# Splitting one batch's result rows 32 to 96 instead of 22 to 106 in an FFT filter and cos-gated MLP kernel

## The chip, the cores and the metric

The kernel runs on one core of a Trainium2 chip. A core has a matrix engine (TensorE, PE in the profile), a vector engine (VectorE, DVE), a scalar engine (ScalarE, ACT), a general one (GpSimd, POOL) and a sync engine (SyncE, SP) that here only issues transfers. Each engine works through its own list of instructions in the order in which the list was built and waits at an instruction until what it needs is there; nothing behind it can pass. Transfers (DMAs) are issued by SP and ACT, in this kernel, and carried out by 16 DMA engines that the two queues share. On-chip memory (SBUF) has 128 partitions. The metric is the device time of one execution in microseconds; less is better.

## The reference, cut to what matters

The input x has 8 batches of 3008 rows by 256 channels. First each batch is filtered along its rows in the frequency domain, then every row goes through a two-layer network with a cosine gate:

```python
X = np.fft.rfft(x, axis=1)                      # 8 x 1505 x 256
Y = X * (filt_r + 1j * filt_i)[None]
y = np.fft.irfft(Y, n=3008, axis=1)             # 8 x 3008 x 256
x = y.reshape(24064, 256)
h = x @ w_in                                    # 256 -> 2048
g = h * np.cos(h)
out = g @ w_out                                 # 2048 -> 256
```

All inputs and the output are float32.

## The kernel before, in words

The transform of length 3008 = 47 x 64 is done by matrix products in four stages. Stage 1 transforms along 47, stages 2 and 3 along 64 (with the filter between them), stage 4 along 47 back. Between the stages the data goes through device memory, because the axis that lies on the partitions changes. `z2` is the array between stages 3 and 4: 8 x 32 blocks (index j) of 96 rows by 256 channels. A unit of stage 4 is up to five half blocks (48 rows each). The list of units begins 5, 5, 1, 5, 5, ..., so the first three units are 11 half blocks and give the 512 rows of the network's first chunk; `n_first` is 3, and `units[n_first][0]` is 11, the half block at which unit 3 begins.

The network works on 47 chunks of 512 rows. For each chunk there are eight steps over the hidden width: `hidden` (L466) multiplies by two 128-wide slices of w_in into the PSUM tile `hp`, of which there are two; `gate` (L476 to L483) forms h cos(h) on VectorE and ScalarE and splits it into a high and a low part, `gh` and `gl`, so that fast fp32r products keep the precision; `project` (L495) multiplies by w_out into the accumulators `acc`. The step after next can write into `hp` only once the gate of the step has read it for the last time, in L479.

The weights come from memory as float32 and are split into such pairs on the chip by `prep_w`: SP loads the tile `raw` (L222; 512 KB, three buffers), ScalarE makes `o` and `r` from it (L231, L233), VectorE `t` (L234), GpSimd joins them (L235), ScalarE casts the high part (L238), GpSimd subtracts for the low part (L239). There are 16 such loads, w_in and w_out by turns for steps 0 to 7. Seven are issued during the first batch's transform, two more (w_out for step 3, w_in for step 4) right after the first chunk's stage 4 loads, and the other seven, beginning with w_out for step 4, while the first chunk is computed.

The first batch is special: nothing else can run until the first chunk's rows exist, so its transform is done in plain float32 in `first1` and `first23`. In the latter, twelve pieces of columns end as a tile `z2t` of 128 partitions by 512 numbers (2 KB a partition). Partition p holds rows of half block p/2, so that 22 partitions are the 11 half blocks of units 0 to 2. Those partitions are written to `z2` at once, by ScalarE's queue (L409). The rest is written by the generator's last step (L412), by SP's queue. That step is run for all twelve pieces in one go, after the stage 4 loads of units 0 to 2 and the two weight loads, and is tied by `issue_after` to the last of those stage 4 loads.

The order of each engine's list is found when the program is built: a scheduler with a timeline of its own costs places the instructions by priority and expected readiness; only the SP engine's order in the first batch is taken as written. `run_due` spreads the next batches' stages over the slots of the network's steps. A change of one transfer's shape can thus reorder instructions far from it.

Of the kernel before, what the change touches and what calls it, by code (L numbers as in the profile page):

```python
# [138 lines left out]
def _units():  # L139


    sizes = [5, 5, 1] + [5] * 99 + [3, 3]
    assert sum(sizes) == B * NB
    starts = np.concatenate([[0], np.cumsum(sizes)])
    return [(int(a), int(n)) for a, n in zip(starts, sizes)]
# [10 lines left out]
def fft_filter_then_cos_glu(ctx: ExitStack, tc: tile.TileContext, ins, outT):  # L156
# [41 lines left out]
    units = _units()  # L198
# [4 lines left out]
    n_first = len(of_chunk[0])  # L203
# [57 lines left out]
    def psum_f(b):  # L261
        if b == 0 and len(done) < n_first:
            if not spare:
                spare.extend(ps_h.tile([P, 2, 512], F32, name="hp")[:, u] for u in range(2))
                spare.append(ps_f.tile([P, 512], F32, name="ps", tag="ps"))
            return spare.pop(0)
        return ps_f.tile([P, 512], F32, name="ps", tag="ps")
# [115 lines left out]
    def first23(i, fas, fbs):  # L383
        cols = slice(512 * i, 512 * i + 512)
        zf = fft.tile([P, 512], F32, name="zf", tag="ld", bufs=5)
        nc.sync.dma_start(zf, z1s[0].rearrange("j (h c k) d -> (j h c) (k d)", h=2, c=2)[:, cols])
        yield
        ps = psum_f(0)
        nc.tensor.matmul(ps, mats["f2"], zf, start=True, stop=True)
        half = slice(2 * (i % 2), 2 * (i % 2) + 2)  # L390
        ya = fft.tile([P, 512], F32, name="ya", bufs=2)
        yb = fft.tile([P, 512], F32, name="yb", tag="sw", bufs=2)
        for y, f in ((ya, fas), (yb, fbs)):
            nc.vector.tensor_tensor(y, ps, f[i // 2][:, half].rearrange("p k d -> p (k d)"), ALU.mult)
        yield
        ps = psum_f(0)
        if i == 0:
            for m, c in (("30", slice(0, D)), ("3", slice(D, 512))):
                nc.tensor.matmul(ps[:, c], mats["f" + m], ya[:, c], start=True, stop=False)
                nc.tensor.matmul(ps[:, c], mats["f" + m + "i"], yb[:, c], start=False, stop=True)  # L400
        else:
            nc.tensor.matmul(ps, mats["f3"], ya, start=True, stop=False)
            nc.tensor.matmul(ps, mats["f3i"], yb, start=False, stop=True)
        tag, bufs = at2[i]
        z = fft.tile([P, 512], F32, name="z2t", tag=tag, bufs=bufs)
        nc.scalar.copy(z, ps)
        to = z2[:NJ].rearrange("j (h c k) d -> (j h c) (k d)", h=2, c=2)[:, cols]
        n0 = 2 * units[n_first][0]
        nc.scalar.dma_start(to[:n0], z[:n0])  # L409
        yield  # L410
        wrote2.setdefault(0, []).append(i)
        nc.sync.dma_start(to[n0:], z[n0:])  # L412
# [112 lines left out]
    with tc.tile_pool(name="first", bufs=12) as first, tc.manual_schedule(engines={mybir.EngineType.SP}):  # L525
        fas, fbs, load, sign = filters(first)
        ones = [first1(i, first) for i in range(NJ // 4)]
        twos = [first23(i, fas, fbs) for i in range(n23)]
        for g in ones:
            next(g)  # L530
# [159 lines left out]
```

## Time and profile before

| what | value |
| --- | --- |
| time, median of 3 runs | 2562.18 us (2557.64 to 2562.96) |
| time of the profiled execution | 2562.1 us |
| its span, first to last instruction | 2560.3 us |
| TensorE busy | 2455.7 us, 96% |
| VectorE busy | 1885.4 us, 74% |
| GpSimd busy | 1430.5 us, 56% |
| ScalarE busy | 1286.1 us, 50% |
| mean granted TensorE clock | 0.979 |

The page gives each engine's busy time as a share of the whole span. From 420 us on TensorE is busy nearly all the time; the gaps are all in the first 420 us, so the views that matter are those of stretches of that part: how busy each engine is there, which engine waits for which, and what SP's and ScalarE's queues issue when. A line that names `SPq` is the time an issuing instruction took on SP's sequencer, not the time its data took to move. In the lists of transfers the second column is that issue time, and KB is the size of one transfer.

### The profile page before, as it was taken

The numbers are of one execution on the slowest core, as the hardware profiler recorded it, in microseconds if no ns is written. First come the engines' busy times: TensorE is split into PE (matmuls) and PEld (weight loads), VectorE is DVE, ScalarE is ACT, GpSimd is POOL, SyncE is SP. The second block draws the span as 40 slices with busy tenths as digits, with TensorE's granted clock in tenths as the row PEclk, the third lists the DMA queues.
The fourth block names the chain that finished last, engine by engine and source line by source line (L and its number), as shares of the span: only waits on it lengthen the run. The fifth ranks groups of instructions, "written<-read, shape, count | busy, mean of one in ns | idle before, by whom it ended". The sixth has DMA issues, their size and how long they took to land.

```text
span 2560.3 us, 29873 instructions
## 1 busy us (share of the span) xinstructions
PE 2455.7 (96%) x10783; PEld 1967.7 (77%) x10783; DVE 1885.4 (74%) x1911; ACT 1286.1 (50%) x1707; POOL 1430.5 (56%) x826
## 2 busy tenths in 40 slices
PE   7369889999999999999999999999999999999999
PEld 2257767888888888888888888888888888888887
DVE  2177987888678877888668886787768886666665
ACT  1355564555545555555545555455554554444443
POOL 1366664656656565656546665566555554444443
PEclk8679999999999999999999999999999999999999
DMA  9253342322322232222313223222312211000000
GB/s 318 72 166 89 129 144 65 119 82 82 85 83 91 90 91 71 93 90 78 93 47 105 86 85 85 79 94 74 100 43 88 99 54 48 24 21 9 17 9 17
DMA packets 134749, 212.27 MB, mean 83 GB/s; under 512 B 12521, under 2 KB 64281, under 8 KB 134601
## 3 DMA queue, kind: packets, MB, share of 16 engines
q1 hardware_dynamic: 82385, 137.97, 17.7%
q10 hardware_dynamic: 52216, 72.39, 8.8%
q8 instruction: 86, 1.41, 0.2%
q14 instruction: 62, 0.51, 0.1%
HBM read 135.33 MB, written 74.97 MB: 82 GB/s over the span
## 4 chain that ended last, share of the span: by engine, by line
PE 82%; DVE 7%; DMA 3%; issue 3%; SPq 2%; ACT 2%; POOL 1%; POOLq 0%; ACTq 0%; DVEq 0%
PE hp L466 36%; PE acc L495 36%; PE ps L435 3%; PE ps L251 2%; PE ps L252 2%; PE ps L253 2%; SPq L412 2%; DVE g L476 1%; DMA xf<-in_x 1%; DVE sw L325 1%; DVE g L477 1%; DMA raw<-in_w_in 1%; ACT g L478 1%; DVE g L479 1%; DVE xo L280 1%
## 5 line engine op out<-in xcount | busy, mean ns | idle before, releaser
L483 POOL TENSOR_TENSOR gl<-g,gh 128x1024 fp32r<-128x1024 f32 x376 | 910.7, 2422 | 825.6 <-ACT gh L481 510.7
L466 PE MATMUL hp<-y,w_in 128*128 128x512 f32 x4512 | 1132.6, 400 | 65.8 <-DVE g L479 63.8
L466 PEld LDWEIGHTS hp<-y,w_in 128*128 128x128 f32 x4512 | 845.3, 190 | 266.6 <-issue 59.8
L495 PE MATMUL acc<-gh,w_out 128*128 128x512 f32 x3008 | 896.9, 396 | 0.7 <-ACT gh L481 0.7
L479 DVE TENSOR_TENSOR g<-g,hp 128x1024 f32<-128x1024 f32 x376 | 457.9, 1218 | 320.6 <-ACT g L478 320.1
L478 ACT ACTIVATE g<-g,half_pi 128x1024 f32<-128x1024 f32 x376 | 433.4, 1153 | 484.2 <-DVE g L477 436.6
L495 PEld LDWEIGHTS acc<-gh,w_out 128*128 128x128 f32 x3008 | 564.0, 188 | 131.1 <-ACT gh L481 1.1
L481 ACT CAST gh<-g 128x1024 fp32r<-128x1024 f32 x376 | 394.9, 1051 | 430.5 <-DVE g L479 424.1
L476 DVE TENSOR_SCALAR g<-hp 128x1024 f32<-128x1024 f32 x376 | 458.8, 1220 | 137.7 <-PE hp L466 130.3
L495 PE MATMUL acc<-gl,w_out 128*128 128x512 f32 x1504 | 549.9, 400 | 1.3 <-POOL gl L483 1.3
L477 DVE SCALAR_TENSOR_TENSOR g<-g,hp 128x1024 f32<-128x1024 f32 x376 | 458.0, 1218 | 9.9
L495 PEld LDWEIGHTS acc<-gl,w_out 128*128 128x128 f32 x1504 | 283.7, 189 | 66.7 <-POOL gl L483 2.1
L452 POOL TENSOR_TENSOR y<-y,y 128x470 fp32r<-128x470 f32 (+29 forms) x142 | 124.9, 884 | 55.8 <-ACT y L449 55.8
L435 PEld LDWEIGHTS ps<-m,z 120*128 120x128 f32 (+1 forms) x816 | 129.3, 192 | 21.0
L314 POOL TENSOR_TENSOR zl<-zf,zh 128x512 fp32r<-128x512 f32 x84 | 111.7, 1330 | 47.8 <-DVE zh L313 24.5
L331 POOL TENSOR_TENSOR yl<-ya,yh 128x512 fp32r<-128x512 f32 x84 | 113.2, 1348 | 42.1 <-ACT yh L330 42.0
L435 PE MATMUL ps<-m,z 120*128 120x120 f32 (+1 forms) x816 | 129.2, 273 | 0.0
L325 DVE SCALAR_TENSOR_TENSOR sw<-sw,sg,f 128x256 f32<-128x256 f32 x168 | 116.9, 735 | 0.0
L313 DVE CAST zh<-zf 128x512 fp32r<-128x512 f32 x84 | 93.1, 1108 | 23.1 <-DMA zf<-z 13.4
L327 DVE TENSOR_TENSOR ya<-ya,sw 128x512 f32<-128x512 f32 x84 | 98.5, 1173 | 0.0
L330 ACT CAST yh<-ya 128x512 fp32r<-128x512 f32 x84 | 51.8, 618 | 91.0 <-DVE ya L327 90.7
L449 ACT CAST y<-y 128x470 fp32r<-128x470 f32 (+29 forms) x150 | 66.9, 456 | 41.3 <-DVE y L443 38.9
(96 smaller groups left out, 1413.3 us busy)
## 6 DMA issues: line engine op xcount, KB each, us to landing
z<-z SPq DMA_DIRECT2D x101, 240.0 KB
out_t<-o ACTq DMA_DIRECT2D x94, 256.0 KB
f<-in_fb SPq DMA_DIRECT2D x84, 256.0 KB
f<-in_fa SPq DMA_DIRECT2D x84, 256.0 KB
zf<-z SPq DMA_DIRECT2D x84, 256.0 KB
z<-z2t ACTq DMA_DIRECT2D x84, 256.0 KB
xf<-in_x SPq DMA_DIRECT2D x42, 480.0 KB
z<-z1t ACTq DMA_DIRECT2D x84, 240.0 KB
```

Source lines behind the costliest of these rows:

```text
L325: nc.vector.scalar_tensor_tensor(sw[:, ks], sw[:, ks], sg[:, 2 * i + k : 2 * i + k + 1], fbt[:, ks], ALU.mult, ALU.mult)
L331: nc.gpsimd.tensor_tensor(yl, ya, yh.bitcast(F32), ALU.subtract)
L435: nc.tensor.matmul(v[:, t, a * r : (a + 1) * r], zf[:, a, t * P : (t + 1) * P], mats[f"m4{a}"][:r, :r], start=True, stop=True)
L452: (nc.vector if i < 2 * n_first else nc.gpsimd).tensor_tensor(yl, part, yh.bitcast(F32), ALU.subtract)
L466: nc.tensor.matmul(hp[:, u], w_in[s][w][:, t, fs], y[:, t], start=(t == 0 and n == 0), stop=(t == NDT - 1 and n == 2))
L476: nc.vector.tensor_scalar(g, h, 0.25, MAGIC, ALU.add, ALU.add)
L477: nc.vector.scalar_tensor_tensor(g, g, MAGIC, h, ALU.subtract, ALU.subtract)
L478: nc.scalar.activation(g, g, AF.Sin, bias=half_pi, scale=-TWO_PI)
L479: nc.vector.tensor_tensor(g, g, h, ALU.mult)
L481: nc.scalar.copy(gh, g)
L483: nc.gpsimd.tensor_tensor(gl, g, gh.bitcast(F32), ALU.subtract)
L495: nc.tensor.matmul(acc, w_out[s][w][:, u, es], g[:, u], start=(s == 0 and u == 0 and n == 0), stop=(s == NFT // 2 - 1 and u == 1 and n == 2))
```

## The change

One number changes. `n0` is the count of partitions of each `z2t` tile that are written at once:

```diff
         to = z2[:NJ].rearrange("j (h c k) d -> (j h c) (k d)", h=2, c=2)[:, cols]
-        n0 = 2 * units[n_first][0]
+        n0 = 32
         nc.scalar.dma_start(to[:n0], z[:n0])
         yield
         wrote2.setdefault(0, []).append(i)
         nc.sync.dma_start(to[n0:], z[n0:])
```

Before, `n0` is 2 x 11 = 22, and 106 partitions are left for L412. After, 32 are written at once by L409, which are the half blocks of units 0 to 3, and 96 are left for L412. The bytes written in all are the same.

Because the scheduler places instructions by expected readiness, the order of the engines' lists changes too. SP's list, from the last two deferred writes on (z_112 is the array `z2`, `z2t` the tile that is written, z_619 and the following ones are the tiles of stage 4's units 3, 4, ..., f the filter tiles, raw the weights before their split). Before:

```order
L412 DMA z_112<-z2t 106x512 [waits DMAHW0_49]
L412 DMA z_112<-z2t 106x512 [waits DMAHW1_49]
L222 DMA raw<-in_w_out 128x2x512 [waits DMAHW2_49,Activation_49]
L306 DMA f<-in_fb 128x512 [waits DMAHW3_49]
L307 DMA f<-in_fa 128x512 [waits DMAHW4_49]
L306 DMA f<-in_fb 128x512 [waits DMAHW5_49]
L307 DMA f<-in_fa 128x512 [waits DMAHW6_49]
L306 DMA f<-in_fb 128x512 [waits DMAHW7_49]
L222 DMA raw<-in_w_in 128x2x512 [waits DMAHW0_49,Activation_49]
L307 DMA f<-in_fa 128x512 [waits DMAHW1_49]
L222 DMA raw<-in_w_out 128x2x512 [waits DMAHW2_49,Activation_49]
L425 DMA z_619<-z_112 120x2x256 [waits DMAHW3_49,PE_49]
```

With the change:

```order
L412 DMA z_112<-z2t 96x512 [waits DMAHW1_49]
L425 DMA z_619<-z_112 120x2x256 [waits DMAHW2_49,PE_49]
L222 DMA raw<-in_w_out 128x2x512 [waits DMAHW3_49,Activation_49]
L306 DMA f<-in_fb 128x512 [waits DMAHW4_49]
L307 DMA f<-in_fa 128x512 [waits DMAHW5_49]
L306 DMA f<-in_fb 128x512 [waits DMAHW6_49]
L307 DMA f<-in_fa 128x512 [waits DMAHW7_49]
L222 DMA raw<-in_w_in 128x2x512 [waits DMAHW0_49,Activation_49]
L306 DMA f<-in_fb 128x512 [waits DMAHW1_49]
L222 DMA raw<-in_w_out 128x2x512 [waits DMAHW2_49,Activation_49]
L425 DMA z_624<-z_112 120x2x256 [waits DMAHW3_49,PE_49]
```

Unit 3's load (z_619), which came after three weight loads and six filter loads, now stands ahead of the first of them; unit 4's (z_624) stands behind three weight loads, as before. The twelve deferred writes keep their place.

TensorE's list, from the end of the network's step 1 (`hp` with w_in_1) to its step 2 (`hp` with w_in_2). Before:

```order
L466 MATMUL hp<-y_555,w_in_1_82 128x512
L466 MATMUL hp<-y_554,w_in_1_83 128x512
L466 MATMUL hp<-y_554,w_in_2_84 128x512 [waits DVE_49,PE_49]
L466 MATMUL hp<-y_555,w_in_2_84 128x512
L466 MATMUL hp<-y_554,w_in_2_85 128x512 [waits Pool_49]
```

With the change (z_619 and z_624 are stage 4 of units 3 and 4, into a PSUM tile `ps` each):

```order
L466 MATMUL hp<-y_554,w_in_1_83 128x512
L435 MATMUL ps<-m_310,z_619 128x120 [waits DMAHW2_49]
L435 MATMUL ps<-m_312,z_619 128x120
L435 MATMUL ps<-m_310,z_619 128x120
L435 MATMUL ps<-m_312,z_619 128x120
L435 MATMUL ps<-m_310,z_624 128x120 [waits DMAHW3_49]
L435 MATMUL ps<-m_312,z_624 128x120
L435 MATMUL ps<-m_310,z_624 128x120
L466 MATMUL hp<-y_554,w_in_2_84 128x512 [waits DVE_49,PE_49]
```

Stage 4 of unit 3 and most of unit 4's now stand between steps 1 and 2, where before step 2 came first and the two units after it. Further on, the lists of all engines differ in the places of single instructions as well.

## The prediction

> **What bounds the kernel now.** I read the stretches first: the busy time of each engine, with the granted clock, the mean busy share of the 16 DMA engines and GB/s in the last three columns.
>
> ```profile
> core 0: us, PE busy (x) PEld busy (x) DVE busy (x) ACT busy (x) POOL busy (x), PEclk, DMA share, GB/s
> 80.00:100.00 20.00, 13.59 (x48) 11.20 (x48) 4.65 (x13) 7.11 (x16) 9.97 (x8) 0.67 0.26 94
> 100.00:120.00 20.00, 0.00 (x0) 0.00 (x0) 0.00 (x0) 0.00 (x0) 0.00 (x0) 0.50 0.13 51
> 120.00:140.00 20.00, 0.00 (x0) 0.00 (x0) 2.65 (x3) 1.83 (x3) 1.38 (x2) 0.50 0.55 192
> 160.00:200.00 40.00, 34.12 (x133) 25.97 (x132) 38.65 (x36) 22.74 (x37) 34.41 (x20) 0.91 0.39 105
> 200.00:300.00 100.00, 97.64 (x441) 78.57 (x440) 83.87 (x86) 53.21 (x75) 65.78 (x40) 1.00 0.36 110
> 300.00:420.00 120.00, 106.14 (x438) 82.46 (x437) 98.63 (x99) 65.57 (x96) 74.72 (x46) 0.94 0.41 123
> 500.00:2560.00 2060.00, 2053.43 (x9182) 1668.59 (x9180) 1556.03 (x1556) 1057.32 (x1364) 1159.12 (x656) 1.00 0.23 70
> ```
>
> After 500 us TensorE is busy 2053 of 2060 us: there it is the bound, and time won before it shifts all of it. Between 100 and 120 us no engine computes at all, and the DMA engines run at 0.13 of their capacity, which is two of sixteen. What keeps them so is in SP's list (start, time of the issuing instructions, count) and in the transfers of that stretch:
>
> ```profile
> 78.62 0.40 SPq L222 DMA_DIRECT2D raw<-in_w_in  x1
> 79.06 43.36 SPq L412 DMA_DIRECT2D z<-z2t  x12
> 122.52 4.30 SPq L222 DMA_DIRECT2D raw<-in_w_out  x1
> ```
>
> ```profile
> DMA packets 509, 1.02 MB, mean 51 GB/s; under 512 B 10, under 2 KB 10, under 8 KB 509
> z<-z2t SPq DMA_DIRECT2D x5, 212.0 KB
> ```
>
> The deferred writes of 106 partitions hold SP for 43.36 us. All twelve are 12 x 106 x 2 KB = 2.61 MB, which at 51 GB/s takes 51 us; SP is held nearly that long, because a new write cannot be issued before the queue has room. Only then comes the next weight load, w_out for step 4. Who waits for it stands in the waits of 76 to 145 us and in ScalarE's and TensorE's rows (the bracket is the idle time before the row, and what ended it):
>
> ```profile
> PE hp L466 <- DVE g L479: 48.2, 1, 48.2
> DVE t L234 <- ACT o L231: 47.4, 2, 47.0
> ACT o L231 <- DMA raw<-in_w_out: 44.6, 2, 44.1
> ```
>
> ```profile
> 91.79 0.62 ACT L238 CAST w_in<-o 128x512 fp32r<-128x512 f32 x1 [1.26 <-POOL o L235]
> 136.55 0.66 ACT L231 ACTIVATE o<-raw 128x512 f32<-128x512 f32 x1 [44.14 <-DMA raw<-in_w_out]
> ```
>
> ```profile
> 87.29 8.27 PE L466 MATMUL hp<-y,w_in 128*128 128x512 f32 x24 [1.97 <-ACT y L449]
> 143.80 4.58 PE L466 MATMUL hp<-y,w_in 128*128 128x512 f32 x12 [48.24 <-DVE g L479]
> ```
>
> Read backwards: TensorE has done steps 0 and 1 (24 products) and needs an `hp` tile back; that hangs on the gate of step 0; in VectorE's list the gate stands behind the weight split's L234, which waits for ScalarE's L231, which waits for the weights, which stand behind the writes in SP's queue. One transfer at the head of SP's list holds four engines. ScalarE is free at 91.79 + 0.62 = 92.41 us and starts at 136.55; TensorE follows 143.80 - 136.55 = 7.25 us later.
>
> **The change part by part.** What is added: the writes at once grow from 22 to 32 partitions. Their count (twelve), place and issuing instructions are the same; they run while the queues are nearly empty. The stage 4 loads of the first chunk wait for the last of them:
>
> ```profile
> 76.63 1.28 SPq L425 DMA_DIRECT2D z<-z  x3
> ```
>
> ```profile
> GB/s 30 0 0 0 0 0 0 0 0 0 0 0 15 179 134 0 0 0 0 0 0 0 0 0 0 0 0 45 149 134 0 0 0 0 0 0 0 0 0 0
> ```
>
> The second row is 72 to 77.5 us in forty slices: the last two writes are the two bursts, and the last burst ends after 30 slices, at 76.1 us, 0.5 us before the waiting load goes out.
>
> I leave that start where it is: 20 KB more is 0.4 us even at the 51 GB/s of two engines, and on more engines less; I take 0, between -0.4 and 0.4.
>
> What is made smaller: 12 x 96 x 2 KB = 2.36 MB in deferred writes. The trace of before has no deferred write of 96 partitions, so I look for the nearest rows: how many engines does a 96-partition tile get? From 3 to 7 us only the loads of 96x512 tiles run on SP's queue, and from 24 to 28 us mostly ScalarE's writes of 96-partition tiles to memory (queue q10):
>
> ```profile
> q1 hardware_dynamic: 616, 1.08, 94.1%
> xf<-in_x SPq DMA_DIRECT2D x8, 192.0 KB
> ```
>
> ```profile
> DMA packets 1246, 1.51 MB, mean 377 GB/s; under 512 B 62, under 2 KB 1150, under 8 KB 1246
> q10 hardware_dynamic: 1132, 1.11, 78.8%
> ```
>
> Both keep all sixteen engines busy (94.1%; 78.8% for q10 with q1 filling the rest). So I expect the deferred writes on all sixteen engines, at 377 GB/s: 2.36 / 0.377 = 6.3 us in place of 51 us. The lower bound is the two engines of now (51 GB/s, 46 us); in between, the rate when the stage 4 and weight loads run together, 255 GB/s:
>
> ```profile
> 79.00:84.00 5.00, 4.28 (x19) 4.07 (x19) 1.39 (x4) 3.15 (x7) 4.39 (x5) 0.50 0.86 255
> 130.00:135.00 5.00, 0.00 (x0) 0.00 (x0) 0.00 (x0) 0.00 (x0) 0.00 (x0) 0.50 0.95 342
> ```
>
> ```profile
> GB/s 0 0 5 87 128 108 353 364 343 261 210 261 215 174 256 144 148 195 241 389 358 369 379 430 358 420 389 420 369 287 164 62 31 51 51 51 51 51 51 51
> ```
>
> The last row is 77 to 85 us in forty slices of 0.2 us: what is queued before the writes has drained after 31 of them, at 83.2 us. From there:
>
> - writes 6.3 us: 89.5 us
> - unit 3's load, now first: 245 KB at the 342 GB/s of the second row: 0.7 us
> - w_out for step 4: 524 KB at 342 GB/s: 1.5 us, so 91.7 us; with the 0.5 us from data to release seen above: 92.2 us.
>
> ScalarE is busy until 92.41 us anyway. Its wait of 44.14 us is then gone and the order of the chain behind it (L231, L234, the two gates' L476 and L477, L238, L478, L479) is as before: step 2 could begin at 92.4 + 7.25 = 99.7 us.
>
> What is moved: seven products of units 3 and 4 now stand ahead of step 2. Rows of ScalarE and TensorE that bear on it:
>
> ```profile
> 87.82 0.68 ACT L233 ACTIVATE r<-raw 128x512 int32<-128x512 uint32 x1
> 88.97 0.67 ACT L233 ACTIVATE r<-raw 128x512 int32<-128x512 uint32 x1
> ```
>
> ```profile
> 148.22 1.94 PE L435 MATMUL ps<-m,z 120*128 120x120 f32 x16
> ```
>
> Unit 3's data is there by 91 us. Unit 4's load is issued behind four filter loads, w_in 5, one more filter load and w_out 5. Those two weight loads wait for `raw` buffers that ScalarE frees by 88.5 and 89.6 us (the two L233 rows, w_out 3 and w_in 4), so they wait for nothing later. Five filter loads of 262 KB, two weights of 524 KB and unit 4's 245 KB are 2.6 MB, 7.6 us at 342 GB/s: 91.7 + 7.6 + 0.5 = 99.8 us, then three products, 3 x 1.94/16 = 0.4 us, doubled for a slow clock: 0.8 us. Step 2 begins at 100.6 us instead of 143.80: **43.2 us** less. Bounds: if nothing is late, 143.80 - 99.7 = 44.1 us; at 255 GB/s all along, the writes take 9.3, the two loads 3.0 and the next 2.6 MB 10.2 us, unit 4 lands at 83.2 + 22.5 + 0.5 = 106.2 us and step 2 begins at 107.0, a gain of 36.8 us.
>
> Behind that, two small terms. Of the sixteen stage 4 products at 148.22 us seven are done in the idle time: 0.8 us. And w_in 6, for which ScalarE waited, need not be as late:
>
> ```profile
> 152.05 0.68 ACT L231 ACTIVATE o<-raw 128x512 f32<-128x512 f32 x1 [3.90 <-DMA raw<-in_w_in]
> ```
>
> Of these 3.90 us I take 1, between 0 and 3.9, as TensorE was not idle at that place and only what follows on VectorE gains. The clock gives nothing: step 2 was slow (4.58 us for 12 products, where twelve of the 24 of steps 0 and 1 take 4.1, also after an idle stretch) and will still come after an idle stretch of some 4 us, and a gap of 1.99 us at 167.49 us already had the same price:
>
> ```profile
> 167.49 4.59 PE L466 MATMUL hp<-y,w_in 128*128 128x512 f32 x12 [1.99 <-DVE g L479]
> ```
>
> What is reordered: from 160 to 420 us VectorE is nearly full (38.65 of 40 us in the first of these rows) and TensorE idles 5.9 + 2.4 + 13.9 = 22.1 us. The work there is the same and starts earlier; its new order may win or lose some of these 22 us. Between -22 (all gone) and +22 (twice as much) I take 0, with 8 either way as likely.
>
> Sum: 43.2 + 0.8 + 1.0 = 45.0 us from the profiled execution's 2562.1 us (span 2560.3 and 1.8 around it), and that execution stands 0.1 us from the median: 2517 us.
>
> On the count of engines the Trainium skill has two voices, both in DMA: Bandwidth & Descriptors. Its table "Specifications" gives eight partitions per engine as a convention; by that 106 partitions would lie on fourteen engines, the slowness would have another cause, and the change would only save bytes, the time of rival B below. Its section "Why a DMA increments its semaphore by 16 and not by 1" has the largest divisor up to 16 of the outer dimension decide: 106 gives two, 96 sixteen. The trace's 0.13 agrees with the second and contradicts the first.
>
> **The rivals.**
>
> A, the forecast: 2517 us, its own range 2508 to 2527.
>
> B, the change doesn't widen the writes: they are slow because of their target or pattern, and 96 partitions cost 96/106 of 106. Then SP is held 43.36 x 96/106 = 39.3 us, 4 us less, and the time is 2558. For it: no write of just this shape is in the trace. Against it: two engines' share exactly, and 96-partition writes at 377 GB/s.
>
> C, the wait goes over to the next weights: SP comes to them 37 us earlier, but they then stand in one burst with filters and unit loads, and steps 4 to 6 wait for w_out 4 to w_in 6 one after another. If each of the four loads is late by the 3.90 us of the row above, 15.6 us are given back: 2533. Against it: the queue has 2.6 MB then, 7.6 us, while TensorE needs w_in 5 only for the fourth step from there.
>
> D, the crowded stretch of 160 to 420 us loses as much as it idles now: 22 us back, 2539. For it: VectorE at 97% there, and a new order on all engines. Against: the same work in the same stretch, with more transfers done ahead.
>
> E, slower: TensorE's list now has unit 4 ahead of step 2. If its load is caught behind w_in 5 and w_out 5, whose buffers ScalarE must free, and that ScalarE work stood behind the gates, every microsecond is TensorE's. It decides from a landing at 143 us; with 151 us, 8 us worse than now, the time is 2570. Against: ScalarE's rows that free the buffers are over at 89.6 us, before any gate.
>
> **How the numbers follow.** A 0.83, B 0.03, C 0.07, D 0.05, E 0.02. The likeliest gives 2517 us. The range, 2506 to 2530, takes in the 8 us of reordering below and above, and above it the slow rate's 36.8 us in place of 43.2. About 0.2% (5 us) is what a measurement of this kernel can tell from no change. A, C and D are faster, 0.95; B is within, 0.03; E is slower, 0.02.
>
> **What would show it.** Right: the L412 rows together take some 8 us or less on SP; the stretch after 83 us shows the DMA engines near full; ScalarE's wait before w_out 4 is under 3 us; step 2 of TensorE begins near 101 us, after products of units 3 and 4; TensorE is full from about 375 us on. Wrong: L412 still above 30 us (B); TensorE's waits move to L222's weights (C); its idle time between 120 and 380 us well above 22 us (D); a long wait of L435 for z ahead of step 2 (E).

## The result, and the profile after

The changed kernel takes 2517.2 us, median of 4 runs (2516.79 to 2519.81), beside 2561.74 us for the kernel before: a ratio of 0.9831, 95% interval 0.9814 to 0.9848. The profiled execution took 2516.79 us with a span of 2515.0 us; the span is 45.3 us shorter.

SP's list of the changed kernel (start, time of the issuing instructions, count):

```profile
78.69 0.40 SPq L222 DMA_DIRECT2D raw<-in_w_in  x1
79.14 8.40 SPq L412 DMA_DIRECT2D z<-z2t  x12
87.66 1.01 SPq L425 DMA_DIRECT2D z<-z  x1
88.77 0.57 SPq L222 DMA_DIRECT2D raw<-in_w_out  x1
```

The twelve deferred writes hold SP for 8.40 us where they held it 43.36 us, and the next weight load goes out at 88.77 us, 33.75 us earlier than before (122.52). The transfers of the changed kernel from 84 to 89 us (packets, MB, share of sixteen engines in the second row):

```profile
DMA packets 1087, 1.92 MB, mean 384 GB/s; under 512 B 153, under 2 KB 153, under 8 KB 1086
q1 hardware_dynamic: 1086, 1.91, 103.6%
z<-z2t SPq DMA_DIRECT2D x6, 192.0 KB, 3.8
```

The share of a little over 100% is to be read as full: all sixteen engines work, at 384 GB/s, where two moved 51 GB/s. The engines that stood still, in stretches of the changed kernel (columns as in the prediction's first table):

```profile
80.00:100.00 20.00, 13.66 (x56) 11.65 (x55) 9.38 (x18) 10.84 (x23) 12.49 (x10) 0.67 0.99 338
100.00:120.00 20.00, 18.04 (x77) 15.10 (x78) 16.73 (x21) 13.99 (x24) 14.57 (x9) 0.80 0.74 204
455.00:2515.00 2060.00, 2053.35 (x9182) 1668.86 (x9180) 1550.29 (x1556) 1057.90 (x1364) 1160.86 (x656) 1.00 0.23 70
```

Between 100 and 120 us TensorE is now busy 18 of 20 us instead of 0. The last 2060 us are as full as before (2053.35 against 2053.43 us busy); they only begin 45 us earlier. ScalarE's and TensorE's rows in the changed kernel that answer to the quoted rows of before:

```profile
94.43 0.67 ACT L231 ACTIVATE o<-raw 128x512 f32<-128x512 f32 x1 [2.06 <-DMA raw<-in_w_out]
107.92 0.68 ACT L231 ACTIVATE o<-raw 128x512 f32<-128x512 f32 x1 [2.06 <-DMA raw<-in_w_in]
```

```profile
94.67 1.05 PE L435 MATMUL ps<-m,z 120*128 120x120 f32 x8
101.96 1.64 PE L435 MATMUL ps<-m,z 120*128 120x120 f32 x6 [6.24 <-DMA z<-z]
103.27 1.63 PE L466 MATMUL hp<-y,w_in 128*128 128x512 f32 x3
```

ScalarE's wait for the weights of step 4 fell from 44.14 to 2.06 us. TensorE's 48.24 us before step 2 became 6.24 us, and what ends it is another transfer: no longer the gate behind the weights, but unit 4's stage 4 load, which the new order has put ahead of step 2. It is nearly a tie: the gate that step 2 needs (L479) is over at 101.53 us, 0.4 us before the load lets TensorE go on. Step 2 begins at 103.27 us instead of 143.80: 40.5 of the 45.3 us are won there, and 4.8 us behind it.

### The profile page after: what moved, and what is told of

Its sections match the earlier page's. It is cut to its first block, busy times and chain, and to the rows that moved or that the text cites. A ratio compares the mean times of both kernels' runs of the same rounds, so it can differ in the third digit from the quotient of the medians.

```text
span 2515.0 us, 29886 instructions
## 1 busy us (share of the span) xinstructions
PE 2453.1 (98%) x10783; PEld 1967.4 (78%) x10783; DVE 1884.4 (75%) x1911; ACT 1286.2 (51%) x1707; POOL 1429.6 (57%) x826
## 4 chain that ended last, share of the span: by engine, by line
PE 82%; DVE 4%; issue 1%; DMA 1%; ACT 1%; POOL 0%; POOLq 0%; ACTq 0%; DVEq 0%; SPq 0%
PE hp L466 37%; PE acc L495 37%; PE ps L435 3%; PE ps L251 2%; PE ps L253 2%; PE ps L252 2%; DVE sw L325 1%; DVE g L476 1%; DVE g L477 1%; DVE g L479 1%; DMA xf<-in_x 0%; DVE zh L313 0%; ACT g L478 0%; DVE xo L280 0%; DVE ya L327 0%
## 5 line engine op out<-in xcount | busy, mean ns | idle before, releaser
L466 PEld LDWEIGHTS hp<-y,w_in 128*128 128x128 f32 x4512 | 842.4, 189 | 219.0 <-issue 12.5
L479 DVE TENSOR_TENSOR g<-g,hp 128x1024 f32<-128x1024 f32 x376 | 457.9, 1218 | 327.0 <-ACT g L478 326.1
L313 DVE CAST zh<-zf 128x512 fp32r<-128x512 f32 x84 | 86.5, 1030 | 25.9 <-DMA zf<-z 14.4
```

The lines of the kernel that those rows point to most:

```text
L466: nc.tensor.matmul(hp[:, u], w_in[s][w][:, t, fs], y[:, t], start=(t == 0 and n == 0), stop=(t == NDT - 1 and n == 2))
L479: nc.vector.tensor_tensor(g, g, h, ALU.mult)
```

## The experiments

Three theories stood against each other. T: the number of DMA engines that a deferred write of so many partitions gets decides. O: the earlier load of unit 3 and the new order of the lists do. V: the bytes that are deferred do. Four splits tell them apart; a fifth question, R, came up on the way.

### 24 at once, 104 deferred

```diff
-        n0 = 32
+        n0 = 24
```

With this split unit 3's rows are again not all among those written at once, and the lists are those of the kernel before: in the trace, TensorE's 10783 products and SP's instructions come in the same order.

> 24 partitions at once, 104 deferred; unit 3's rows (22 to 31) are then not all written at once, and the order of the TensorE, VectorE and GpSimd lists is that of the kernel before, row for row. Theory T (the number of DMA engines on which a deferred write lies decides, and 104 gets 13 of 16): 2.56 MB at 13/16 of 377 GB/s, 8.3 us; the deferred writes hold SP for 8 to 11 us instead of 43; step 2 of TensorE begins at 99 to 103 us; time 2513 to 2524 us. Rival O (the gain comes from unit 3's earlier load and the new order of the lists): 2560 us, since neither is there. Rival V (only the bytes of the deferred writes count): 104/106 of the writes, 2561 us.

Measured: 2517.05 us (2515.44 to 2519.26), ratio 0.9833 [0.9817, 0.985]. SP's list and the transfers from 84 to 89 us:

```profile
79.33 9.84 SPq L412 DMA_DIRECT2D z<-z2t  x12
```

```profile
DMA packets 899, 1.64 MB, mean 328 GB/s; under 512 B 101, under 2 KB 101, under 8 KB 898
q1 hardware_dynamic: 898, 1.63, 85.3%
```

and TensorE's step 2:

```profile
101.97 5.11 PE L466 MATMUL hp<-y,w_in 128*128 128x512 f32 x12 [6.13 <-DVE g L479]
```

Thirteen of sixteen engines would be 81.3%; the queue shows 85.3%, with 328 GB/s. Two partitions fewer in each deferred write, the old order, and the whole gain: T holds, O and V fall. Step 2 begins 1.3 us earlier than in the change; no unit load stands ahead of it here, and what ends the wait is the gate (L479) again.

### 34 at once, 94 deferred

```diff
-        n0 = 32
+        n0 = 34
```

> 34 partitions at once, 94 deferred: fewer bytes deferred than in the change, unit 3's rows all written at once and its load ahead of the next weights, as in the change. Theory T: 94 = 2 x 47 lies on two engines again; SP is held 43.36 x 94/106 = 38.5 us, and the time is 2553 to 2560 us. Rivals O and V: 2515 to 2520 us, as the change or a little better.

Measured: 2565.9 us (2563.35 to 2568.86), ratio 1.0025 [1.0014, 1.0035]: the whole gain is gone although less is deferred than in the change. SP's list and the transfers from 100 to 120 us:

```profile
85.25 38.10 SPq L412 DMA_DIRECT2D z<-z2t  x12
```

```profile
q1 hardware_dynamic: 510, 1.02, 13.1%
z<-z2t SPq DMA_DIRECT2D x7, 188.0 KB
```

Two engines, 38.10 us of SP, as T had it (38.5). The time is 6 us beyond T's upper end, and TensorE's row at the start of stage 4 says why (the answering row of the change behind it, from that kernel's own list):

```profile
85.93 2.06 PE L435 MATMUL hp<-m,z 120*128 120x120 f32 x8 [9.20 <-DMA z<-z]
```

```profile
79.59 2.06 PE L435 MATMUL hp<-m,z 120*128 120x120 f32 x8 [5.75 <-DMA z<-z]
```

The first chunk's stage 4 begins 6.3 us late. The writes at once have 34 = 2 x 17 partitions, and those too now crawl. These are the transfers from 70 to 86 us in forty slices (from about 72 to 82 us nearly all of them are ScalarE's writes), and then the L409 rows of this kernel and of the change (the two times at the end are the starts of the first and of the last write):

```profile
GB/s 170 99 129 48 48 50 48 53 52 51 46 36 36 31 41 51 41 0 0 0 0 0 31 31 41 51 26 26 36 41 51 15 0 0 18 202 333 279 228 225
```

```profile
L409 ACTq DMA_DIRECT2D z<-z2t x12: 231/232/478, 39.6 to 80.1; - x12
L409 ACTq DMA_DIRECT2D z<-z2t x12: 308/309/329, 40.8 to 74.8; - x12
```

The writes mostly move at no more than some 50 GB/s, the rate of two engines. But 5.3 of the 6.3 us are lost before the last of them is issued, and only some 1 us behind it: the pieces themselves come later. Earlier on, ScalarE waits 6.81 us for the load of one piece (`zf`), where the change waits 3.88, and from 54 to 58 us the engines move 171 GB/s where they move 409 in the change. So the narrow writes seem to hold up the loads that share the engines with them; that step is read from these rows and was not tested alone. The expectation had looked at the deferred half of the split alone.

### 27 at once, 101 deferred

```diff
-        n0 = 32
+        n0 = 27
```

> 27 partitions at once, 101 deferred; TensorE's, VectorE's and GpSimd's lists in the order of the kernel before. Theory T: 101 is prime and lies on one engine, half of the 51 GB/s; 2.48 MB take 97 us instead of 51, so the weights behind them come some 44 to 48 us later than before: 2602 to 2612 us. Rivals O and V: 2558 to 2562 us.

Measured: 2604.74 us (2603.94 to 2605.55), ratio 1.0176 [1.0156, 1.0197]. SP's list, the transfers from 100 to 120 us, and TensorE:

```profile
78.82 85.23 SPq L412 DMA_DIRECT2D z<-z2t  x12
```

```profile
DMA packets 252, 0.51 MB, mean 26 GB/s; under 512 B 2, under 2 KB 2, under 8 KB 252
q1 hardware_dynamic: 252, 0.51, 6.6%
```

```profile
189.32 5.46 PE L466 MATMUL hp<-y,w_in 128*128 128x512 f32 x12 [94.06 <-DVE g L479]
```

One engine of sixteen (6.6%), half the rate, twice the stall: the suspected cost is doubled by five partitions fewer in each deferred write, in the order of the kernel before (TensorE's and SP's rows in the trace are again the same). The time lies in T's range. This also closes the question whether something later would have hidden the stall: 45.5 us more before step 2 are 45.0 us more in the time.

### 22 and 106, the 106 in two pieces

```diff
-        nc.sync.dma_start(to[n0:], z[n0:])
+        nc.sync.dma_start(to[n0:32], z[n0:32])
+        nc.sync.dma_start(to[32:], z[32:])
```

Here on the kernel before, so `n0` is 22.

> 22 partitions at once and 106 deferred as in the kernel before, but each deferred write is issued as two, of 10 and 96 partitions, so that 24 issues replace 12. Theory T: 10 and 16 engines, 2.6 MB in some 7.5 us; 24 issues of 0.35 to 0.5 us hold SP 9 to 13 us; time 2516 to 2526 us. Rival V: 2562 us. Rival O: 2562 us, since unit 3's rows are deferred.

Measured: 2504.16 us (2502.97 to 2505.24), ratio 0.9783 [0.9769, 0.9798]. The 24 issues hold SP from 78.28 to 90.77 us, 12.5 us (the first and the last of their rows):

```profile
78.28 0.40 SPq L412 DMA_DIRECT2D z<-z2t  x1
90.46 0.31 SPq L413 DMA_DIRECT2D z<-z2t  x1
```

T, against O and V, holds once more: the old split loses nothing once its deferred part is issued in widths that spread. But the time is 12 us below T's lower end and 13 us below the change. Step 2 is not what is faster:

```profile
103.17 4.84 PE L467 MATMUL hp<-y,w_in 128*128 128x512 f32 x12
```

It begins where it does in the change (103.27). The rest of the span, from there on, is 2501.6 - 103.17 = 2398.4 us, against 2515.0 - 103.27 = 2411.7 in the change. The lists' order differs between the two. Hence a further pair of theories for what lies behind step 2, T: worth single microseconds, and R: the order into which the scheduler falls is worth ten and more.

### 48 at once, 64 at once, an earlier weight load, and twice 48 deferred

Four more kernels, in which every write has a multiple of sixteen partitions:

```diff
-        n0 = 32
+        n0 = 48
```

> 48 partitions at once, 80 deferred, both on 16 engines; the loads of units 3 and 4 both stand ahead of the next weights, so the 6.24 us for which TensorE waited for unit 4 before step 2 should shrink. Theory T (width decides, the rest is worth single microseconds): step 2 at 99 to 102 us, time 2512 to 2519 us. Rival R (the order into which the scheduler falls in the filter stretch of 100 to 440 us is worth ten and more us either way): anything from 2500 to 2530 us, with step 2 at the same place.

```diff
-        n0 = 32
+        n0 = 64
```

> 64 partitions at once, 64 deferred, 1.57 MB in some 4.2 us; three unit loads and three weight loads ahead of the filters. T: step 2 at 98 to 102 us, time 2510 to 2519 us. R: 2500 to 2530 us; if having unit loads and weights ahead of the filter loads is what made the split writes fast, then near 2504 us.

```diff
-EARLY_W, JUST_W = 9, 5
+EARLY_W, JUST_W = 10, 5
```

> The change, and one more weight load (w_out for step 4) asked for early, so that it stands behind the first deferred write instead of the twelfth. T: ScalarE's wait of 2.06 us for it goes, and step 2 begins 1 to 3 us earlier unless unit 4's load is waited for: 2513 to 2519 us. R: 2500 to 2530 us.

```diff
-        nc.sync.dma_start(to[n0:], z[n0:])
+        nc.sync.dma_start(to[n0:80], z[n0:80])
+        nc.sync.dma_start(to[80:], z[80:])
```

> The change, with each deferred write of 96 partitions issued as two of 48, both on 16 engines: the same bytes, engines and split, twelve issues more (24 of 0.3 to 0.45 us), and another order of all lists, which has unit loads and weights ahead of the filters. T: as the change, at most 3 us worse: 2516 to 2520 us. R: far from it although nothing but the order and twelve issues differ, near the 2504 us of the split into 10 and 96, whose order is the most alike.

Measured: 2502.04 us (ratio 0.9779 [0.9762, 0.9795]) for 48 at once, 2501.86 (0.9781 [0.9766, 0.9795]) for 64, 2510.71 (0.9813 [0.9798, 0.9828]) for the earlier weight load, 2515.39 (0.9829 [0.9815, 0.9844]) for twice 48. All kernels together, with the start of step 2 and what is left of the profiled span behind it (us; "SP held" from the first deferred write's issue to the end of the last):

| at once / deferred | SP held | step 2 begins | span | left behind step 2 |
| --- | --- | --- | --- | --- |
| 22 / 106 (before) | 43.4 | 143.80 | 2560.3 | 2416.5 |
| 32 / 96 (the change) | 8.4 | 103.27 | 2515.0 | 2411.7 |
| 24 / 104 | 9.8 | 101.97 | 2516.1 | 2414.1 |
| 34 / 94 | 38.1 | 148.13 | 2561.7 | 2413.6 |
| 27 / 101 | 85.2 | 189.32 | 2602.2 | 2412.9 |
| 22 / 10 + 96 | 12.5 | 103.17 | 2501.6 | 2398.4 |
| 48 / 80 | 9.3 | 103.53 | 2499.5 | 2396.0 |
| 64 / 64 | 9.2 | 102.00 | 2500.1 | 2398.1 |
| 32 / 96, weights earlier | 10.4 | 100.84 | 2512.6 | 2411.8 |
| 32 / 48 + 48 | 13.3 | 100.12 | 2516.1 | 2416.0 |

Among the kernels whose deferred writes spread, step 2 begins between 100.1 and 103.5 us, and where it begins earliest (twice 48) the time is not the best. The 16.6 us between the shortest and the longest of these spans lie behind step 2. There the deferred writes are long over, and the work is the same 10783 products. The kernels of 22, 24 and 27 at once, whose TensorE order is the same, lie within 3.6 us of one another in the last column although their stalls differ by 87 us; the others, each with an order of its own, reach 20 us below the longest. That is why R is the reading that is left. It is reached by exclusion: no run changes the order alone.

The expectations fared as follows. T's part, that the rest is worth single microseconds, fails by 10 us for 48 at once, by 8 for 64, by 2 for the earlier weight load, and by less than 1 for twice 48. R's range of 2500 to 2530 us takes in the first three, but it is wide. For twice 48 R said that the time would come near the 2504 us of the split whose order is most like it; that fails by 11 us. With it fails that unit loads and weights ahead of the filters make the fast group, since twice 48 has them so, too. The medians form a group of 2501.9 to 2504.2 and one of 2510.7 to 2517.2 us; executions of one kernel differ by 2 to 6 us, and the profiled one of the earlier weight load is the slowest of its four.

Where the microseconds lie can be seen in the stretch before the full last 2060 us. First the change, then 48 at once, each in the 220 us before its last 2060:

```profile
235.00:335.00 100.00, 91.56 (x403) 72.81 (x402) 91.21 (x95) 56.13 (x80) 64.12 (x39) 1.00 0.33 104
335.00:455.00 120.00, 113.91 (x498) 90.40 (x498) 95.43 (x102) 64.23 (x94) 74.78 (x47) 0.97 0.42 125
```

```profile
219.50:319.50 100.00, 93.71 (x411) 74.15 (x410) 90.49 (x96) 57.88 (x83) 67.97 (x42) 1.00 0.35 115
319.50:439.50 120.00, 119.30 (x540) 96.63 (x539) 95.29 (x99) 64.67 (x92) 75.10 (x46) 1.00 0.40 116
```

And the page's first rows, again the change, then 48 at once:

```profile
PE 2453.1 (98%) x10783; PEld 1967.4 (78%) x10783; DVE 1884.4 (75%) x1911; ACT 1286.2 (51%) x1707; POOL 1429.6 (57%) x826
```

```profile
PE 2446.4 (98%) x10783; PEld 1963.8 (79%) x10783; DVE 1880.7 (75%) x1911; ACT 1286.5 (51%) x1707; POOL 1431.3 (57%) x826
```

TensorE idles less (14.5 us in the two rows of the change, 7.0 us in those of 48 at once), and the same 10783 products take 6.7 us less over the whole execution. The other 8.8 of the 15.5 us between the spans are idle time. The 6.7 us go with the clock: its mean is 0.988 in the change and 0.991 in 48 at once, and 0.3% of 2453 us is some 7 us, as an estimate. A gap can bring a slow clock with it: in the change, behind 1.71 us of idle time at 385.46 us, sixteen stage 4 products take 3.77 us at a granted clock of 0.50, where sixteen of 48 at once take 1.94 at a clock of 1.00 (at 97.77 us). Not every gap does: behind 2.59 us at 249.24 us the clock stays at 1.00, and the change's first row above idles 8.4 us at 1.00. What decides it no run here shows. Nor was it tried one by one which of the moved rows opens or closes the gaps. So it also stays open whether 48 or 64 partitions at once as such have a part in it: their order cannot be had with the change's widths, or the other way round.

48 and 64 at once are the fastest versions here, some 15 us below the change.

## Why the prediction was right, point by point

**The bound.** The stall of all engines was SP's queue behind the narrow writes. The split of 27 and 101 doubles it and 24 and 104 removes it in the old order; both are shown by runs. SP's hold is not all of it: in the kernel before the weights' load went out at 122.52 us and was used at 136.55, since the writes already queued had until about 134 us to go, as an estimate (the prediction's 83.2 us, from which they run alone, and 51). Whether the load would have passed them on ScalarE's queue was not tried.

**The writes on sixteen engines.** Predicted 377 GB/s and 6.3 us; measured 384 GB/s and full engines. SP's 8.40 us is a little above the "8 us or less" that was to show it. The five widths were seen as follows: 101 on one engine (6.6%, 26 GB/s), 94 and 106 on two (13.1%, 51 GB/s), 104 on thirteen (85.3%, 328 GB/s), 96 on sixteen (103.6%, 384 GB/s). The rule by the largest divisor (the Trainium skill, DMA: Bandwidth & Descriptors, section "Why a DMA increments its semaphore by 16 and not by 1") gives these counts, and the traces agree with it at all five widths. The convention of eight partitions per engine (the Trainium skill, DMA: Bandwidth & Descriptors, section "Specifications") would give thirteen, twelve, fourteen, thirteen and twelve in this order (101, 94, 106, 104, 96), and the traces agree with it at 104 alone.

**Step 2 at 100.6 us, 43.2 us won.** Measured 103.27 and 40.5: the mechanism, down to unit 4's load as the last thing waited for, is as worked out, and the terms ahead of it are too small by 2.7 us. Some 2.2 us were lost by the first weights: w_out for step 4 was used at 94.43 instead of 92.2 us. From there on the sum held: unit 4 ended TensorE's wait 7.5 us later, at 101.96 us, where 7.6 us were worked out at 342 GB/s. These are the transfers of the changed kernel from 88 to 103 us, in forty slices of 0.375 us:

```profile
GB/s 344 344 344 344 230 216 292 227 147 208 303 371 388 377 355 361 350 350 410 382 393 415 393 410 404 410 410 399 399 382 221 221 238 238 276 265 265 243 235 300
```

The rate drops at 89.5 us, where the prediction had the writes end, and stays at 147 to 303 GB/s for seven slices. The sum has the two loads behind the writes run at 342 GB/s without a pause; at these rates their 0.77 MB take some 0.8 us longer, as an estimate. The other 1.4 us, and why the engines slowed there, are not accounted for. The last 0.5 us are products: six of unit 4 stand ahead of step 2 and take 1.3 us, where the sum has three at 0.8.

**Behind step 2, 0.8 + 1.0 us.** Measured 4.8 us. The first term counted wrongly: each of the seven instructions ahead of step 2 in TensorE's list is two products in the trace, so that fourteen of the sixteen (8 + 6 in the rows above) had moved: 1.94 x 14/16 = 1.7 us instead of 0.8. The second, ScalarE's later wait for w_in 6, shrank by 3.90 - 2.06 = 1.8 us; how much of that reached TensorE is not shown. The rest, 1.3 us or more, is less than the 3.6 us by which kernels of one order differ there.

**The reordering, 0 with 8 either way.** For this change 0 was right: the old order with 104 deferred gives the same time (2517.05 against 2517.2). The 8 us were too narrow for other splits: their orders, with step 2 at much the same time, are 13 to 16 us shorter behind it than the change. The outer bound of 22 us held. That the median came out within 1 us of 2517 is therefore partly luck: the missing 2.7 us at step 2 and the 3.0 us too many behind it cancel.

**The rivals.** B (no widening) is what 94 and 101 deferred show and what 96 does not. C (the wait goes to the next weights): ScalarE waits 2.06 us twice, not 3.90 four times. D (the crowded stretch eats the gain) did not come: from 120 to 375 us TensorE idles 17.8 us. Its ground, VectorE at 97%, was read from the first of the three rows alone; the other two have 84% and 82%. TensorE was not quite full from 375 us on, as the list of signs had it: it idles 3.7 us until 455. E's place was well seen, its price was not: unit 4's load did end TensorE's wait before step 2, at 102 us and not at 143.

## What to carry to other kernels

Look at how many partitions a transfer has before looking at its bytes: a busy share of 0.13 with nothing else running is two engines of sixteen, and a count of 96 or 104 instead of 106 was worth some 43 to 45 us of 2562 here. A narrow transfer also holds the queue that issues it, and everything behind it in that list: an issuing instruction of several microseconds is the sign. Where a tile is split, both parts need a count that spreads, and once the stall is gone, a few neighbouring splits are worth timing, because here splits that all spread still differed by as much as a third of the gain, most likely through the order that the scheduler fell into.

## What the runs showed of the hardware that was not expected

A queue that is full of narrow writes held its issuer nearly for the whole time that the data took: 85.23 of some 95 us for one engine's 12 x 101 partitions (2.48 MB at 26 GB/s), 43.36 of some 51 for two engines' 12 x 106. The twelve writes on sixteen engines held it for 8.40 us. The rate per engine stayed between 24 and 26 GB/s at each width (26 at one, 51 at two, 328 at thirteen, 384 at sixteen). And 34 partitions instead of 32 in the twelve writes at once of 64 KB, which looked free, put off the start of the next stage by 6.3 us.
